# Copying the far maxima directly behind the pairing, with the mark passes and a dense piece moved ahead of the scores

## The chip, the cores and the metric

The kernel runs on one core of a Trainium2 chip. A core has five engines that run side by side, each through its own list of instructions in order: TensorE (PE, matrix products; PEld is its loading of weights), VectorE (DVE), ScalarE (ACT), GpSimd (POOL) and SyncE (SP, which issues transfers here). The metric is the time of one execution in microseconds of device time; lower is better.

## The reference

An attention with a top-32 mask per row, and behind it a feed-forward layer with squared ReLU:

```python
# q, k, v: (8 batches, 8 heads, 576 rows, 64)
scores = q @ k.T / 8
kth = 32nd largest of each row of scores
scores = where(scores >= kth, scores, -1e9)
attn = softmax(scores)
x = (attn @ v) as (4608 tokens, 512)
h = maximum(x @ w_in, 0)         # 512 -> 2048
out = (h * h) @ w_out            # 2048 -> 512
```

## The kernel before

The rows of scores are worked on in 144 steps of two tiles of 128 rows each (`steps`; most steps hold the same chunk of rows of two heads, 16 of them the last 64 rows of four heads). A tile has 576 columns. For each step, in the kernel's names:

- `scores(u)`: TensorE computes the scores into two PSUM tiles, `sc_b` (columns 288 to 575 of the scores) first and then `sc_a` (columns 0 to 287). Each of these tiles has two banks of 512 numbers, one for each of the two tiles of rows, and uses the first 288 of them. ACT copies both to `s` in SBUF (line 202).
- `far` is the place of columns 288 to 431 in the two banks of `sc_b`, behind the scores. It holds the upper half of the pairwise maxima.
- `split(u)`: DVE pairs the two halves of a row: `tops` is the maximum of each pair (line 227). In a step that is *lent* the minima are left to POOL (`small_mins`), and the upper half of the maxima is copied to `far` by ACT (line 209). In a step that isn't lent, DVE writes `far` itself (line 229) and computes half of the minima too. A planner's debts of POOL and ACT decide which steps are lent.
- `join(u)`: DVE pairs `far` with the lower half of `tops` (line 242); in some steps the minima of that are left to POOL (`joint_mins`).
- `topk(u, rounds)`: DVE takes the largest eight of a window and strikes them out, four times (lines 274 and 278). The eighth of the fourth round is the threshold.
- `below(u, x)`: ACT's mark pass, one for each tile of rows (line 320): what lies below the threshold gets a positive mark.
- `exps(u)`: ACT's exponentials (line 328); `mask(u)`: POOL adds the marks to them as integers (line 324); `turn(u)`: a transposing transfer.
- `products(u)`, `invert` and `place(u)`: weighted sums of `v` on TensorE (line 389), reciprocals on DVE (lines 394 and 400), and the scaled copy to `x_tok` on ACT (line 417).
- `dense(u, x)`: one piece of the feed-forward layer on TensorE (lines 494 and 517), or a piece without use where none is ready (line 539); what ACT and POOL do with a piece is issued later, between the exponentials (`flush`).

Every instruction is pinned, so each engine's order is the order in which the code issues it. The steps overlap: in a step u from 12 on (`lead` is 2), the code finishes the top-32 search of step u, pairs the rows of step u + 2, scores those of step u + 3, and works on the marks and exponentials of step u − 1. Where a tile is used by two engines, the framework adds semaphores from the tile's accesses. Steps 9 to 11 (`DEEP` is 9) change over from a lead of 1, in an order of their own. From step 125 on (`Z`) another loop, at line 741, runs the last steps; it has `split` before `topk`, and `ahead`, which issues the scores, behind `mask` and `turn`.

The main loop's order in a step, before the change, cut to the calls that matter:

```python
below(u - 1, 0)
split(u + 2)
ahead(u + 3)            # scores(u + 3), with the copies
topk(u, (0,))
place(f - 1)            # f = u - 4
joint_mins(u + 1)
small_mins(u + 2)
dense(u, 0)
below(u - 1, 1)
topk(u, (1,)); topk(u, (2,)); topk(u, (3,))
join(u + 2)
exps(u - 1); mask(u - 1); turn(u - 1)
dense(u, 1); products(u - 3); prepare(u)
```

Of the kernel before, what the change touches and what calls it, by code (L numbers as in the profile page):

```python
# [17 lines left out]
AF = mybir.ActivationFunctionType  # L18
# [4 lines left out]
def kernel(  # L23
# [9 lines left out]
    nc = tc.nc  # L33
# [10 lines left out]
    HALF, QUAR = S // 2, S // 4  # L44

    def pin(ins):
        tc.keep_in_program_order(ins)
        return ins
# [3 lines left out]
    def owe(**more):  # L52
        for e, t in more.items():
            debt[e] += t

    def pass_step():
        for e in debt:
            debt[e] = max(0.0, debt[e] - {"G": 5.9, "A": 6.1}[e])
# [38 lines left out]
    far = sc[1][:, :, HALF:HALF + QUAR]  # L97
# [82 lines left out]
    Z, DEEP = U - 19, 9  # L180
# [6 lines left out]
    st = {}  # L187


    def scores(u):  # L190
        for j in (1, 0):
            rest = steps[u][0][1] == 4
            for x, g in ((0, 0), (1, 1), (0, 1), (1, 0)) if rest else ((0, steps[u][0][2]), (1, steps[u][1][2])):
                i, c, _ = steps[u][x]
                qkT = prep[i][0]
                r = slice(64 * g, 64 * g + 64)
                pin(nc.tensor.matmul(out=sc[j][r if rest else slice(0, 128), x, 0:HALF], lhsT=qkT[r, 0, c * 128:min(S, (c + 1) * 128)],  # L197
                                     rhs=qkT[r, 1, j * HALF:(j + 1) * HALF], start=True, stop=True))
        s = scp.tile([128, 2, S], f32, name="s", bufs=5)

        def copy(j):
            pin(nc.scalar.activation(s[:, :, j * HALF:(j + 1) * HALF], sc[j][:, :, 0:HALF], AF.Copy))  # L202
        st[u] = {"s": s}
        copy(1)
        if u < 2:
            st[u]["rest"] = lambda: copy(0)
        else:
            if "lent" in st[u - 1]:
                pin(nc.scalar.activation(far, st[u - 1]["tops"][:, :, QUAR:HALF], AF.Copy))  # L209
            copy(0)  # L210
        for i, c, a in steps[u]:
            qk_left[i] -= 1
# [4 lines left out]
    def split(u):  # L217
        d = st[u]
        lend = (2 < u < U - 20 and debt["G"] < 4.9 and debt["A"] < 5.4) or Z < u < U - 5
        cat = d["cat"] = scp.tile([128, 2, S], f32, name="cat", bufs=3)  # L220
        tops = d["tops"] = scp.tile([128, 2, HALF], f32, name="tops", bufs=2)
        one, two = sc[0][:, :, 0:HALF], d["s"][:, :, HALF:S]
        tt = nc.vector.tensor_tensor
        if lend:
            owe(G=1.22, A=0.4)
            d["lent"] = True
            pin(tt(tops[:, :, :], one, two, op=ALU.max))  # L227
        else:
            pin(tt(far, one[:, :, QUAR:HALF], two[:, :, QUAR:HALF], op=ALU.max))
            pin(tt(tops[:, :, 0:QUAR], one[:, :, 0:QUAR], two[:, :, 0:QUAR], op=ALU.max))  # L230
        if not lend:
            pin(tt(cat[:, :, HALF + QUAR:S], one[:, :, QUAR:HALF], two[:, :, QUAR:HALF], op=ALU.min))
        if "rest" in d:
            d.pop("rest")()

    def join(u):
        d = st[u]
        d["joint"] = "lent" in d and DEEP + 4 <= u < Z + 2 and debt["G"] < 4.5
        if d["joint"]:
            owe(G=1.6)  # L240
        for lo, op in ((0, ALU.max), (QUAR, ALU.min))[0:1 if d["joint"] else 2]:
            pin(nc.vector.tensor_tensor(d["cat"][:, :, lo:lo + QUAR], far, d["tops"][:, :, 0:QUAR], op=op))  # L242

    def joint_mins(u):
        d = st[u]
        if d["joint"]:
            at, tops = d["cat"][:, :, QUAR:HALF].bitcast(i32), d["tops"][:, :, :].bitcast(i32)
            pin(nc.gpsimd.tensor_tensor(at, tops[:, :, 0:QUAR], tops[:, :, QUAR:HALF], op=ALU.add))  # L248
            pin(nc.gpsimd.tensor_tensor(at, at, d["cat"][:, :, 0:QUAR].bitcast(i32), op=ALU.subtract))

    def small_mins(u):
        d = st[u]
        n = HALF if "lent" in d else QUAR
        s, at = d["s"], d["cat"][:, :, HALF:HALF + n].bitcast(i32)
        pin(nc.gpsimd.tensor_tensor(at, s[:, :, 0:n].bitcast(i32), s[:, :, HALF:HALF + n].bitcast(i32), op=ALU.add))  # L255
        pin(nc.gpsimd.tensor_tensor(at, at, d["tops"][:, :, 0:n].bitcast(i32), op=ALU.subtract))  # L256
# [61 lines left out]
    def below(u, x):  # L318
        d = st[u]
        pin(nc.scalar.activation(marks[u % 2][:, x, :], d["s"][:, x, :], AF.Relu, bias=d["m"][3][:, x, 7:8], scale=-1.0))  # L320
# [21 lines left out]
    def flush():  # L342
        while late:
            late.pop(0)()
# [191 lines left out]
    def idle_piece(n=KH, name="dn_ps", bufs=1):  # L536
        hp = ps_one.tile([128, 512], f32, name=name, bufs=bufs)
        for kh in range(n):
            pin(nc.tensor.matmul(out=hp[:, :], lhsT=id_h[:, :], rhs=fill[:, :], start=(kh == 0), stop=(kh == n - 1)))
# [3 lines left out]
    def piece():  # L543
        flush()
        turn_of[0] ^= 1
        for q_ in ((ups, downs), (downs, ups))[turn_of[0]]:
            if q_:
                q_.pop(0)()
                return True
        return False  # L550

    def dense(u, x):
        for go in ripe.pop(u, ()):
            go()
        if moves and x == 1:
            flush()
            moves.pop(0)(u)
        if x == 1 and not ups and 0 < len(downs) <= 6 and u < 100:
            flush()
            idle_piece(2, "gen", 2)  # L560
            return
        for n in range(2 if len(ups) + len(downs) > 24 or (x == 1 and u >= 100 and u % 3 == 0 and len(ups) + len(downs) > 4) else 1):
            if not piece() and n == 0 and u < U:
                idle_piece()
# [66 lines left out]
    join(0)  # L631
    small_mins(0)
    scores(1)


    def ok(w):
        return 0 <= w < U
# [11 lines left out]
    def ahead(w):  # L649
        if w < U:  # L650
            for i, c, a in steps[w]:
                while coming <= i or (coming == i + 1 and soon):
                    prepare(u)
            scores(w)

    for u in range(Z):
        f = u - 4
        lead = 2 if u > DEEP + 2 else 1
        pass_step()
        owe(A=4.5, G=3.0)  # L660
        if u > 0:
            below(u - 1, 0)
        if u == 0:
            topk(0, (0, 1))
            split(1)
            join(1)
            topk(0, (2, 3))
        elif not DEEP < u < DEEP + 3:
            split(u + lead)
        if not DEEP < u < DEEP + 3:  # L670
            ahead(u + 1 + lead)
        if u > 0:
            topk(u, (0,))
        if u == DEEP + 2:
            join(u + 1)
            split(u + 2)
            ahead(u + 3)
        if ok(f) and f % 2:
            invert_two(f)
        if ok(f - 1):  # L680
            place(f - 1)
        if checks:
            note()
        if lead > 1:
            joint_mins(u + 1)
        if u == DEEP + 2:
            small_mins(u + 2)
        elif u != DEEP + 1:
            small_mins(u + lead)
        dense(u, 0)  # L690
        if u > 0:
            below(u - 1, 1)
            topk(u, (1,))
            if u == DEEP + 1:
                join(u + 1)
            topk(u, (2,))
            if u == DEEP + 1:
                split(u + 2)
                small_mins(u + 2)
                ahead(u + 3)  # L700
            topk(u, (3,))
            if u == DEEP:
                join(u + 1)
                split(u + 2)
            elif u != DEEP + 1:
                join(u + 2 if u > DEEP else u + 1)
            exps(u - 1)
            mask(u - 1)
            turn(u - 1)
        flush()  # L710
        if u == Z - 1:
            assert u % 2 == 0
            products(u - 3)
            expo(u, 0)
            expo(u, 1)
        else:
            dense(u, 1)
            flush()
            products(u - 3)
        if u == DEEP:  # L720
            small_mins(u + 2)
            ahead(u + 3)
        for _ in range(2 if u < 8 or u in (U - 22, U - 19) else 1):
            prepare(u)
        if 1 < u < 24 and not ups and not downs:
            idle_piece(2)
        turn_x(u)
        if w_casts and u >= 3:
            w_casts.pop(0)()
        if w_loads and u >= 1:  # L730
            w_loads.pop(0)()
# [57 lines left out]
    u = U - 2  # L789
# [67 lines left out]
    u = U - 1  # L857
# [187 lines left out]
```

## Time and profile before

| what | us |
|---|---|
| median of three runs | 907.39 (905.39 to 907.63) |
| the profiled execution | 905.09 |
| its span, from the first to the last instruction | 903.2 |
| VectorE busy | 865.9 |
| ScalarE busy | 827.1 |
| GpSimd busy | 809.7 |
| TensorE busy | 738.5 |

The profile is of one execution. Busy times count the engine's own instructions, without waits. In rows of a timeline the first two numbers are the start and the length in us; a bracket gives idle time before the instruction and what ended it. In rows of waits stand the total of the waits, how many there were and the longest.

### The profile page before, as it was taken

The numbers are of one execution on the slowest core, as the hardware profiler recorded it, in microseconds if no ns is written. First come the engines' busy times: TensorE is split into PE (matmuls) and PEld (weight loads), VectorE is DVE, ScalarE is ACT, GpSimd is POOL, SyncE is SP. The second block draws the span as 40 slices with busy tenths as digits, with TensorE's granted clock in tenths as the row PEclk, the third lists the DMA queues.
The fourth block names the chain that finished last, engine by engine and source line by source line (L and its number), as shares of the span: only waits on it lengthen the run. The fifth ranks groups of instructions, "written<-read, shape, count | busy, mean of one in ns | idle before, by whom it ended". The sixth has DMA issues, their size and how long they took to land.

```text
span 903.2 us, 19114 instructions
## 1 busy us (share of the span) xinstructions
PE 738.5 (82%) x5474; PEld 435.8 (48%) x5474; DVE 865.9 (96%) x3503; ACT 827.1 (92%) x1691; POOL 809.7 (90%) x756
## 2 busy tenths in 40 slices
PE   7888777887778878787888878787888877978986
PEld 3444335455445444454544444455555544545644
DVE  5999889999999999999999999999999999999994
ACT  3988889999999999999999999899999999999973
POOL 4789879999999999999999999999999998899851
PEclk8989889999999898999999999999999998999989
DMA  5597674454566565445554455554546555334431
GB/s 118 136 205 155 167 170 90 99 96 104 100 122 119 96 110 117 88 99 113 108 113 95 101 108 109 109 113 94 112 97 123 114 111 114 68 71 63 89 82 42
DMA packets 326880, 98.00 MB, mean 109 GB/s; under 512 B 318960, under 2 KB 319216, under 8 KB 326768
## 3 DMA queue, kind: packets, MB, share of 16 engines
q1 hardware_dynamic: 325424, 96.28, 52.1%
q8 instruction: 45, 0.74, 0.4%
q10 hardware_dynamic: 1344, 0.43, 0.2%
q14 instruction: 67, 0.55, 0.2%
HBM read 36.70 MB, written 9.44 MB: 51 GB/s over the span
## 4 chain that ended last, share of the span: by engine, by line
DVE 46%; PE 15%; ACT 15%; POOL 9%; issue 8%; DMA 4%; SPq 2%; DVEq 0%; ACTq 0%; POOLq 0%
DVE m L274 18%; DVE cat L278 13%; DVE cat L242 6%; DVE tops L227 6%; ACT s L202 5%; PE sc_b L197 3%; PE av_ps L389 3%; PE dn_ps L517 3%; POOL cat L255 2%; POOL h L503 2%; PE sc_a L197 2%; ACT marks_a L320 2%; POOL cat L256 2%; ACT marks_b L320 1%; ACT x_tok L417 1%
## 5 line engine op out<-in xcount | busy, mean ns | idle before, releaser
L274 DVE MAX8 m<-cat 128x8 f32<-128x104 f32 (+3 forms) x1152 | 437.1, 420 | 0.0
L278 DVE MATCH_REPLACE8 cat<-m,cat 128x104 f32<-128x104 f32 (+2 forms) x864 | 261.2, 309 | 0.0
L256 POOL TENSOR_TENSOR cat<-cat,tops 128x576 int32<-128x576 int32 (+1 forms) x144 | 191.7, 1331 | 13.2 <-DVE tops L230 2.1
L255 POOL TENSOR_TENSOR cat<-s 128x576 int32<-128x576 int32 (+1 forms) x144 | 191.6, 1330 | 7.0 <-ACT s L202 6.6
L389 PEld LDWEIGHTS <-wT 128*128 128x128 bf16 (+3 forms) x1600 | 98.2, 100 | 143.0 <-issue 76.9
L517 PE MATMUL dn_ps<-w_out,h 128*128 128x512 bf16 x560 | 160.0, 417 | 5.2 <-ACT wide L527 5.2
L197 PE MATMUL sc_b<-qkT 64*128 64x288 f32 (+1 forms) x640 | 129.2, 487 | 40.5 <-DVE cat L242 30.5
L503 POOL TENSOR_TENSOR h<-rl 128x512 bf16<-128x512 f32 x140 | 145.0, 1040 | 7.8 <-ACT rl L500 5.4
L494 PEld LDWEIGHTS <-w_in 128*128 128x128 bf16 x1344 | 114.5, 101 | 50.7 <-issue 23.9
L494 PE MATMUL gen<-xT,w_in 128*128 128x256 bf16 (+1 forms) x1088 | 133.0, 271 | 2.6 <-ACT rl L500 1.6
L197 PE MATMUL sc_a<-qkT 64*128 64x288 f32 (+1 forms) x640 | 123.2, 471 | 1.3 <-DVE tops L227 1.3
L242 DVE TENSOR_TENSOR cat<-sc_b,tops 128x288 f32<-128x288 f32 x256 | 104.1, 443 | 10.5 <-ACT sc_b L209 8.5
L320 ACT ACTIVATE marks_a<-s,m 128x576 bf16<-128x576 f32 x144 | 112.0, 786 | 0.4
L202 ACT ACTIVATE s<-sc_b 128x576 f32<-128x576 f32 x144 | 94.1, 654 | 19.5 <-PE sc_b L197 15.0
L320 ACT ACTIVATE marks_b<-s,m 128x576 bf16<-128x576 f32 x142 | 109.2, 776 | 0.1
L202 ACT ACTIVATE s<-sc_a 128x576 f32<-128x576 f32 x144 | 91.7, 637 | 7.9 <-PE sc_a L197 5.3
L227 DVE TENSOR_TENSOR tops<-sc_a,s 128x576 f32<-128x576 f32 x126 | 94.0, 746 | 1.3 <-POOL cat L248 1.0
L517 PEld LDWEIGHTS <-h 128*128 128x128 bf16 x560 | 51.3, 104 | 83.3 <-issue 43.5
L197 PEld LDWEIGHTS sc_b<-qkT 64*128 64x128 f32 (+1 forms) x640 | 50.6, 186 | 71.8 <-DVE cat L242 40.0
L500 ACT ACTIVATE rl<-gen 128x512 f32<-128x512 f32 x140 | 83.3, 595 | 1.7 <-PE gen L494 1.2
L197 PEld LDWEIGHTS sc_a<-qkT 64*128 64x128 f32 (+1 forms) x640 | 61.5, 196 | 40.2 <-DVE tops L227 21.1
L328 ACT ACTIVATE w_two_a<-s,low 128x576 bf16<-128x576 f32 x96 | 71.5, 774 | 0.8
(136 smaller groups left out, 1170.5 us busy)
## 6 DMA issues: line engine op xcount, KB each, us to landing
q_raw<-in_q_dram SPq DMA_DIRECT2D x64, 128.0 KB, 3.0
v_raw<-in_v_dram SPq DMA_DIRECT2D x64, 128.0 KB, 3.1
k_raw<-in_k_dram SPq DMA_DIRECT2D x62, 128.0 KB, 3.0
out_dram<-wide SPq DMA_DIRECT2D x31, 256.0 KB, 2.7
h<-in_moe_w_in_dram SPq DMA_DIRECT2D x8, 512.0 KB, 5.2
h<-in_moe_w_out_dram SPq DMA_DIRECT2D x8, 512.0 KB, 4.3
out_dram<-wide SPq DMA_DIRECT2D x9, 128.0 KB, 2.4
q_raw<-in_q_dram SPq DMA_DIRECT2D x32, 32.0 KB, 2.8
```

The lines of the kernel that those rows point to most:

```text
L197: pin(nc.tensor.matmul(out=sc[j][r if rest else slice(0, 128), x, 0:HALF], lhsT=qkT[r, 0, c * 128:min(S, (c + 1) * 128)], rhs=qkT[r, 1, j ...
L202: pin(nc.scalar.activation(s[:, :, j * HALF:(j + 1) * HALF], sc[j][:, :, 0:HALF], AF.Copy))
L227: pin(tt(tops[:, :, :], one, two, op=ALU.max))
L242: pin(nc.vector.tensor_tensor(d["cat"][:, :, lo:lo + QUAR], far, d["tops"][:, :, 0:QUAR], op=op))
L255: pin(nc.gpsimd.tensor_tensor(at, s[:, :, 0:n].bitcast(i32), s[:, :, HALF:HALF + n].bitcast(i32), op=ALU.add))
L256: pin(nc.gpsimd.tensor_tensor(at, at, d["tops"][:, :, 0:n].bitcast(i32), op=ALU.subtract))
L274: pin(nc.vector.max(out=m[r][:, x, :], in_=cat[:, x, at]))
L278: pin(nc.vector.match_replace(out=cat[:, x, at], in_to_replace=m[r][:, x, :], in_values=cat[:, x, at], imm_value=NEG))
L320: pin(nc.scalar.activation(marks[u % 2][:, x, :], d["s"][:, x, :], AF.Relu, bias=d["m"][3][:, x, 7:8], scale=-1.0))
L494: pin(nc.tensor.matmul(out=hp[:, n * n_rows:(n + 1) * n_rows], lhsT=w_in[:, kh, (f0 + n) * 128:(f0 + n + 1) * 128], rhs=xt(kh), start=(kh ...
L503: squares.append(lambda by: pin(by.tensor_mul(h2, flat, flat)))
L517: pin(nc.tensor.matmul(out=op[:, :], lhsT=held["h2"][:, f, c * 128:(c + 1) * 128], rhs=w_out[:, f, :], start=(f == 0), stop=(f == NF - 1)))
```

## The change

Three things move; no instruction is added or taken out.

- The copy of the upper maxima to `far` is issued in `split`, directly behind the pairing, for all lent steps from 11 on. It stood in `scores` of the next step, between the copies of `sc_b` and `sc_a`.
- From step 12 on both mark passes stand at the head of the step.
- From step 12 on `joint_mins`, `small_mins` and the first dense piece stand directly behind `split`, ahead of the scores.

```diff
         if u < 2:
             st[u]["rest"] = lambda: copy(0)
         else:
-            if "lent" in st[u - 1]:
+            if "lent" in st[u - 1] and u - 1 < DEEP + 2:
                 pin(nc.scalar.activation(far, st[u - 1]["tops"][:, :, QUAR:HALF], AF.Copy))
             copy(0)
...
             pin(tt(tops[:, :, :], one, two, op=ALU.max))
+            if u >= DEEP + 2:
+                pin(nc.scalar.activation(far, tops[:, :, QUAR:HALF], AF.Copy))
...
         if u > 0:
             below(u - 1, 0)
+        if lead > 1:
+            below(u - 1, 1)
...
         elif not DEEP < u < DEEP + 3:
             split(u + lead)
+        if lead > 1:
+            joint_mins(u + 1)
+            small_mins(u + 2)
+            dense(u, 0)
         if not DEEP < u < DEEP + 3:
             ahead(u + 1 + lead)
...
-        if lead > 1:
-            joint_mins(u + 1)
         if u == DEEP + 2:
             small_mins(u + 2)
-        elif u != DEEP + 1:
+        elif lead == 1 and u != DEEP + 1:
             small_mins(u + lead)
-        dense(u, 0)
+        if lead == 1:
+            dense(u, 0)
         if u > 0:
-            below(u - 1, 1)
+            if lead == 1:
+                below(u - 1, 1)
             topk(u, (1,))
```

## The prediction

> **What bounds the kernel now.** I read the page first, then the busy times of stretches of the span.
>
> ```profile
> span 903.2 us, 19114 instructions
> ## 1 busy us (share of the span) xinstructions
> PE 738.5 (82%) x5474; PEld 435.8 (48%) x5474; DVE 865.9 (96%) x3503; ACT 827.1 (92%) x1691; POOL 809.7 (90%) x756
> ```
>
> VectorE (DVE) has the most work, but ScalarE (ACT) and GpSimd (POOL) are close. The shares are diluted by the start and the end, so I asked for the stretch from 75 to 850 us, which holds nearly everything that the change touches (columns: stretch, length, busy PE, PEld, DVE, ACT, POOL with counts, granted clock, DMA share, GB/s).
>
> ```profile
> 75.00:850.00 775.00, 633.99 (x4715) 376.95 (x4713) 761.62 (x3097) 741.61 (x1523) 736.74 (x666) 0.93 0.53 106
> ```
>
> There DVE is idle for 775.00 − 761.62 = 13.4 us and ACT for 775.00 − 741.61 = 33.4 us. So DVE sets the pace and ACT follows closely: whatever lengthens ACT's in-order list by more than 33.4 us in all makes ACT the bound. How much could the change win? The far copy is L209, and DVE's only large wait in this stretch is for it, in the join of L242:
>
> ```profile
> DVE cat L242 <- ACT sc_b L209: 8.5, 10, 2.3
> ```
>
> Ten waits, 8.5 us. That is the most that an earlier far copy can give.
>
> Next, one step on ACT, in order of time (start, length).
>
> ```profile
> 401.62 0.77 ACT L320 ACTIVATE marks_b<-s,m 128x576 bf16<-128x576 f32 x1
> 402.29 0.64 ACT L202 ACTIVATE s<-sc_b 128x576 f32<-128x576 f32 x1
> 402.96 0.41 ACT L209 ACTIVATE sc_b<-tops 128x288 f32<-128x288 f32 x1
> 403.31 0.63 ACT L202 ACTIVATE s<-sc_a 128x576 f32<-128x576 f32 x1
> 403.84 0.51 ACT L417 ACTIVATE x_tok<-av_ps,shares 128x64 bf16<-128x64 f32 x2
> 404.23 0.78 ACT L320 ACTIVATE marks_b<-s,m 128x576 bf16<-128x576 f32 x1
> ```
>
> Nothing here waits: each starts before the last has quite ended. The same step on DVE (the join, then the pairing of the next rows) and on TensorE (scores, then a dense piece):
>
> ```profile
> 399.66 0.43 DVE L242 TENSOR_TENSOR cat<-sc_b,tops 128x288 f32<-128x288 f32 x1
> 400.01 0.74 DVE L227 TENSOR_TENSOR tops<-sc_a,s 128x576 f32<-128x576 f32 x1
> ...
> 405.14 0.80 DVE L242 TENSOR_TENSOR cat<-sc_b,tops 128x288 f32<-128x288 f32 x2
> ...
> 405.86 0.74 DVE L227 TENSOR_TENSOR tops<-sc_a,s 128x576 f32<-128x576 f32 x1
> ```
>
> ```profile
> 400.14 0.76 PE L197 MATMUL sc_b<-qkT 64*128 64x288 f32 x4 [0.28 <-DVE cat L242]
> 400.81 0.76 PE L197 MATMUL sc_a<-qkT 64*128 64x288 f32 x4
> 401.50 1.04 PE L517 MATMUL dn_ps<-w_out,h 128*128 128x512 bf16 x4
> ```
>
> Pairing starts at 400.01 and again at 405.86: a step of 5.85 us. Its tops are ready at 400.75, ACT's first mark pass starts only at 401.62: ACT runs behind DVE and finds its inputs ready.
>
> Now the point that decides. The scores of sc_b go to columns 0 to 287 of a bank; "far" is columns 288 to 431 of the same bank. Still TensorE starts those scores 0.05 us after the join, which only reads far, has ended (399.66 + 0.43 = 400.09). That is the rule over the whole kernel (idle time before line 197, times):
>
> ```profile
>   DVE cat L242: 70.5, 90
> ```
>
> And where DVE writes far itself, in a step that isn't lent, the scores come 0.05 us behind the end of that write (376.22 + 0.47 = 376.69), before the next two DVE operations:
>
> ```profile
> 376.22 0.47 DVE L229 TENSOR_TENSOR sc_b<-sc_a,s 128x288 f32<-128x288 f32 x1
> ...
> 376.74 0.76 PE L197 MATMUL sc_b<-qkT 64*128 64x288 f32 x4
> ```
>
> So in this program whoever touches far holds back the scores of sc_b, and the scores hold back whoever comes next, although no byte is shared. The Trainium skill, "PSUM — Partial Sum Buffer", section "PSUM bank collisions raise a hardware error", goes further than these two rows: any two engines on one bank must be ordered by semaphores, writes and reads alike, even for different columns. No row here shows scores behind an ACT write to far; by that rule they wait for it too and the time would be the forecast's 1021, and if only shared bytes counted, the 897 of the first rival.
>
> **The change, part by part.** No instruction is added or removed; the order on ACT, PE and POOL changes.
>
> *The far copy.* Before, ACT ran: sc_b copy of the next scores, far copy, sc_a copy. The scores had been computed long before, under the mark pass. Now the far copy stands before the scores in program order, so I expect the chain: far copy, then scores of sc_b, then the sc_b copy, and ACT has nothing between the first and the last. The list on ACT becomes mark, mark, far copy, (wait), sc_b copy, sc_a copy, x_tok. From the start of the far copy to the start of the sc_a copy: 0.41 for the copy, 0.05 to release TensorE, 0.76 for the scores of sc_b, 0.05 back to ACT, and 0.67 until the sc_a copy can start, since sc_a's scores end 401.57 − 400.90 = 0.67 us behind sc_b's. Sum 1.94 us. Before, sc_b copy, far copy and sc_a copy took 403.31 − 402.29 = 1.02 us to the same point. The step's ACT list grows by 0.92 us. From below: if the sc_a copy could follow after 0.53 us (403.31 to 403.84), it is 0.78.
>
> How often:
>
> ```profile
> 75.00:850.00 775.00, 48.92 (x118) 0.93 0.53 106
> ```
>
> This row is line 209's alone: 118 far copies in the stretch. Three of them belong to steps 9 to 11, whose order is another one; I count 115: 115 × 0.92 = 105.8 us (from below 115 × 0.78 = 89.7).
>
> *Steps of remainders.* By the list of steps, 16 of the 144 score the last 64 rows of four heads with twice the matmuls; two lie before step 9 and two follow a step that isn't lent, which leaves 12. One of them:
>
> ```profile
> 476.97 2.19 PE L197 MATMUL sc_b<-qkT 64*64 64x288 f32 x8 [1.97 <-DVE cat L242]
> 478.94 1.72 PE L197 MATMUL sc_a<-qkT 64*64 64x288 f32 x8
> ```
>
> The scores of sc_b take 2.19 instead of 0.76, and sc_a's end 480.66 − 479.16 = 1.50 behind them instead of 0.67: 1.43 + 0.83 = 2.26 us more on ACT. This row is a long one; I take 2.0: 12 × 2.0 = 24 us. From below 0.
>
> *Scores at a lower clock.* The row of the stretch grants 0.93, and such a group looks like this:
>
> ```profile
> 413.10 1.33 PE L197 MATMUL sc_b<-qkT 64*128 64x288 f32 x4
> 414.22 1.17 PE L197 MATMUL sc_a<-qkT 64*128 64x288 f32 x4
> ```
>
> If a stretch at half clock makes 0.93 out of 1, its share is 14%, and each such step costs 0.57 for sc_b and 0.49 for sc_a's later end (1.16 instead of 0.67): at most 115 × 0.14 × 1.06 = 17 us. These groups are hidden today and the rows at 400.14 and 376.74 have 0.76, so I take half, 8 us; the ends are 0 and 17.
>
> *What ACT gets back.* Once ACT is the bound, its waits of today fall into the new one. In the stretch (busy, mean ns | idle before and its releasers, then two waits):
>
> ```profile
> L202 ACT ACTIVATE s<-sc_b 128x576 f32<-128x576 f32 x130 | 85.1, 654 | 11.7 <-PE sc_b L197 7.2 <-ACT marks_a L320 2.0 <-issue 1.5
> L202 ACT ACTIVATE s<-sc_a 128x576 f32<-128x576 f32 x129 | 82.1, 636 | 5.0 <-PE sc_a L197 5.0
> ```
>
> ```profile
> ACT w_out L590 <- DMA h<-in_moe_w_out_dram: 7.0, 2, 3.9
> ...
> ACT qkT L132 <- PE gen L128: 1.4, 4, 0.5
> ```
>
> 11.7 + 5.0 + 1.4, and half of the 7.0, since data that a later ACT asks for has had more time to land: 21.6 us, say 22. The ends are 17 (the copies' waits alone) and 33 (all of ACT's idle time).
>
> *The mark pass moved ahead.* Its maxima are there, as ACT trails DVE, so it waits for nothing. It delays both copies by 0.67 us. The sc_b copy is needed by the pairing at 405.86 and ended at 402.93, 2.9 us early. Behind the second mark (0.67), the far copy (0.41) and the wait (0.86) it ends 1.94 us later, 1.0 us early. That cover shrinks with each step in which ACT falls behind: it costs nothing extra, it is where the 0.92 reaches DVE.
>
> *The dense piece ahead of the scores.* 1.04 us on TensorE. It runs while ACT does its two mark passes and the far copy (0.67 + 0.67 + 0.41 = 1.75 us), so scores don't wait for it: nothing. If that cover is gone, up to 1.04 us a step. Behind the x_tok copies TensorE has the weighted sums and transposes, then this piece; ACT has two exponentials, up to two activations of pieces, two marks and the far copy, which is longer.
>
> *POOL's two passes.* They now stand ahead of the overflow notes, eight small groups; their order against the masks and squares is kept. Nothing. No DMA is issued by anything moved, so SP's queue passes nothing.
>
> *The win.* At most the 8.5 us of the join's waits; it is DVE's idle time, and DVE no longer sets the end. I count nothing.
>
> The profiled execution took 905.1 us, 1.9 more than its span, and 2.3 less than the median of the runs. Sum: 905.1 + 105.8 + 24 + 8 − 22 = 1020.9, **1021 us**. Check against ACT alone: (741.6 + 33.4 − 22 + 137.8) = 891 us for the stretch, against DVE's 762: ACT is the bound by far. From below: 905.1 + 89.7 − 33 = 962. From above: 905.1 + 105.8 + 12 × 2.26 + 17 − 17 = 1038.
>
> **The rivals.** *The scores don't wait for the far copy.* If the program orders ACT's write and the matmul by columns, the far copy comes earlier or as early as now, ACT gains no wait, and the join's 8.5 us go: 905.1 − 8.5 = 896.6. For it: the join reads far in steps where scores are still to come. Against it: the 90 waits for the join and the row at 376.74, both without a shared byte. It decides if a matmul on sc_b starts while line 209 still runs. Chance 5%.
>
> *ACT's slack takes the wait.* ACT idles 33.4 us over some 130 steps, 0.26 us a step; a wait of up to that would be free and the time would stay 905. It takes a wait of 0.92 to shrink below 0.3, which the 0.76 of the scores alone excludes unless TensorE starts early. Chance 3%.
>
> *The clock falls.* If TensorE's new gaps make half clock more frequent, say in 40% of the time instead of 14%, the scores cost 115 × 0.26 × 1.06 = 32 us more: 1053, and more with a larger share. For it: the granted clock isn't 1 today. Against it: the gaps per step are under 1 us, and today's waits of TensorE at x_tok are as long or longer. The Trainium skill, "TensorE: Matmul & The Clock Gate", section "A second HAM failure mode: psum-queue depth-cycling", has frequent short idle times between groups of matmuls as a cause of an oscillating clock; by that this rival would hold, with its 1053, and today's 0.93 neither shows nor excludes it. Chance 8%.
>
> **How the numbers follow.** The forecast, 1021, has 84%. Its own ends are 962 and 1038; the clock rival adds up to 1053. The range is 960 to 1055. A measurement here tells about 0.3% from no change, 2.7 us: faster 0.05 (the first rival), same 0.03 (the second), slower 0.92 (the forecast and the clock).
>
> **What would show it.** In the profile of the changed kernel: the scores of sc_b wait for ACT at line 209's copy, about a hundred times; the sc_b copy of ACT idles some 100 us for TensorE's scores, against 11.7; DVE has a new idle time of 80 to 130 us in the join or the pairing, released by ACT's sc_b copy or the scores, and its share falls to about 85%; the step grows from 5.9 to about 6.8 us; the granted clock stays at 0.9 or above. I am wrong if line 209's copy and the scores overlap, if ACT's idle time stays at some 33 us in this stretch, or if the far copy's wait is for the pairing instead.

## The result: 13% slower, and the profile after

The changed kernel takes 1028.74 us (median of four, 1024.22 to 1033.26) against 907.51 us for the kernel before in the same comparison: a ratio of 1.134 (95% interval 1.127 to 1.141), 121 us more. The profiled execution took 1024.2 us. In line numbers after, the far copy is L229, the join L244; the pairing is still L227 and the copies of the scores L202.

The page of the changed kernel, its first lines:

```profile
span 1022.2 us, 18810 instructions
## 1 busy us (share of the span) xinstructions
PE 753.5 (74%) x5397; PEld 450.2 (44%) x5474; DVE 880.0 (86%) x3503; ACT 826.0 (81%) x1691; POOL 811.9 (79%) x756
```

ACT has the work that it had (826.0 after 827.1 us), and DVE nearly (880.0 after 865.9). So the loss is nearly all idle time: over the span ACT's went from 76.1 to 196.2 us and DVE's from 37.3 to 142.2 us, in a span that is 119.0 us longer. The question is who waits first. One step on ACT, which answers to the six rows shown of before:

```profile
462.56 1.43 ACT L322 ACTIVATE marks_b<-s,m 128x576 bf16<-128x576 f32 x2
463.89 0.40 ACT L229 ACTIVATE sc_b<-tops 128x288 f32<-128x288 f32 x1
465.21 0.65 ACT L202 ACTIVATE s<-sc_b 128x576 f32<-128x576 f32 x1 [0.92 <-PE sc_b L197]
465.75 0.65 ACT L202 ACTIVATE s<-sc_a 128x576 f32<-128x576 f32 x1
466.29 0.52 ACT L419 ACTIVATE x_tok<-av_ps,shares 128x64 bf16<-128x64 f32 x2
```

and on TensorE, with a dense piece that ended before the wait:

```profile
461.87 1.03 PE L519 MATMUL dn_ps<-w_out,h 128*128 128x512 bf16 x4
464.35 0.76 PE L197 MATMUL sc_b<-qkT 64*128 64x288 f32 x4 [1.45 <-ACT sc_b L229]
464.94 0.65 PE L197 MATMUL sc_a<-qkT 64*128 64x288 f32 x4
```

and on DVE:

```profile
465.89 0.82 DVE L244 TENSOR_TENSOR cat<-sc_b,tops 128x288 f32<-128x288 f32 x2 [1.05 <-ACT s L202]
466.63 0.75 DVE L227 TENSOR_TENSOR tops<-sc_a,s 128x576 f32<-128x576 f32 x1
```

ACT's far copy ends at 464.29, the scores start 0.06 us later, and the sc_b copy starts 0.92 us after the far copy's end. ACT does nothing in between. TensorE has nothing to do either: its dense piece is long done. The chain of before (the scores early, under a mark pass) has turned into far copy, scores, copy, one behind the other.

The four longest waits of the kernel (engine, line and what released it: us in total, times, longest):

```profile
PEld sc_b L197 <- ACT sc_b L229: 227.8, 118, 3.6
PE sc_b L197 <- ACT sc_b L229: 178.1, 112, 3.1
ACT s L202 <- PE sc_b L197: 135.0, 123, 2.4
DVE cat L244 <- ACT s L202: 99.5, 97, 2.9
```

They are the chain in its order: scores behind the far copy, 118 times; ACT behind the scores, 135.0 us; DVE's join behind ACT, 99.5 us. The wait of 8.5 us that the join had for the far copy is gone, and 99.5 us have come in its place.

The last link is easy to overlook. The join reads `far` and `tops`; it needs nothing of the sc_b copy. Yet it starts at 465.89, 0.03 us after that copy's end (465.21 + 0.65), and all 94 joins of the kernel that had idled for over 0.3 us start as close behind an sc_b copy. So the place of `far` ties two engines to the scores of sc_b: TensorE doesn't write them before the far copy, and DVE doesn't read `far` before ACT has read them.

The stretch of the moved copies now goes from 75 to 960 us:

```profile
75.00:960.00 885.00, 644.10 (x4559) 385.60 (x4622) 764.55 (x3047) 729.90 (x1501) 729.45 (x656) 0.90 0.46 93
```

ACT is idle for 885.00 − 729.90 = 155.1 us there, against 33.4 us in the stretch of before: 121.7 us more, the size of the loss. DVE's idle time went from 13.4 to 120.5 us. By the groups of ACT in this stretch, the two copies of the scores now hold 143.3 us of it, after 16.7:

```profile
L202 ACT ACTIVATE s<-sc_b 128x576 f32<-128x576 f32 x128 | 83.2, 650 | 130.8 <-PE sc_b L197 130.1 <-ACT marks_a L322 0.3
L202 ACT ACTIVATE s<-sc_a 128x576 f32<-128x576 f32 x128 | 83.0, 648 | 12.5 <-PE sc_a L197 12.4
```

### The profile page after: what moved, and what is told of

Read it like the earlier page. It is cut to its first block, busy times and chain, and to the rows that moved or that the text cites. A ratio compares the mean times of both kernels' runs of the same rounds, so it can differ in the third digit from the quotient of the medians.

```text
span 1022.2 us, 18810 instructions
## 1 busy us (share of the span) xinstructions
PE 753.5 (74%) x5397; PEld 450.2 (44%) x5474; DVE 880.0 (86%) x3503; ACT 826.0 (81%) x1691; POOL 811.9 (79%) x756
## 4 chain that ended last, share of the span: by engine, by line
ACT 37%; PE 22%; DVE 19%; POOL 12%; issue 8%; DMA 1%; SPq 1%; ACTq 0%; POOLq 0%; DVEq 0%
PE sc_b L197 9%; ACT s L202 7%; DVE m L276 6%; ACT marks_a L322 6%; ACT marks_b L322 6%; DVE cat L280 4%; DVE tops L227 4%; PE sc_a L197 4%; ACT rl L502 4%; POOL cat L257 3%; PE av_ps L391 3%; ACT sc_b L229 3%; DVE cat L244 3%; POOL cat L258 2%; ACT w_two_b L330 2%
## 5 line engine op out<-in xcount | busy, mean ns | idle before, releaser
L197 PE MATMUL sc_b<-qkT 64*128 64x288 f32 (+1 forms) x640 | 134.8, 509 | 187.0 <-ACT sc_b L229 178.1
L202 ACT ACTIVATE s<-sc_b 128x576 f32<-128x576 f32 x144 | 93.6, 650 | 137.0 <-PE sc_b L197 135.0
L244 DVE TENSOR_TENSOR cat<-sc_b,tops 128x288 f32<-128x288 f32 x256 | 106.1, 451 | 100.1 <-ACT s L202 99.5
L519 PE MATMUL dn_ps<-w_out,h 128*128 128x512 bf16 x496 | 142.0, 405 | 14.2 <-issue 6.3
L496 PE MATMUL gen<-xT,w_in 128*128 128x256 bf16 (+1 forms) x1088 | 144.6, 284 | 8.5 <-ACT rl L502 7.0
L391 PEld LDWEIGHTS <-wT 128*128 128x128 bf16 (+3 forms) x1600 | 102.5, 103 | 99.7 <-issue 59.9
L496 PEld LDWEIGHTS <-w_in 128*128 128x128 bf16 x1344 | 117.1, 104 | 61.1 <-issue 41.1
L197 PE MATMUL sc_a<-qkT 64*128 64x288 f32 (+1 forms) x640 | 119.9, 463 | 0.0
L202 ACT ACTIVATE s<-sc_a 128x576 f32<-128x576 f32 x144 | 93.3, 648 | 15.8 <-PE sc_a L197 12.7
L322 ACT ACTIVATE marks_a<-s,m 128x576 bf16<-128x576 f32 x144 | 105.7, 794 | 0.0
L227 DVE TENSOR_TENSOR tops<-sc_a,s 128x576 f32<-128x576 f32 x126 | 94.5, 750 | 12.3 <-ACT s L202 8.9
L322 ACT ACTIVATE marks_b<-s,m 128x576 bf16<-128x576 f32 x142 | 102.4, 769 | 0.1
L197 PEld LDWEIGHTS sc_a<-qkT 64*128 64x128 f32 (+1 forms) x640 | 68.3, 205 | 26.2 <-issue 3.4
```

Of the source, the lines that this page charges most:

```text
L496: pin(nc.tensor.matmul(out=hp[:, n * n_rows:(n + 1) * n_rows], lhsT=w_in[:, kh, (f0 + n) * 128:(f0 + n + 1) * 128], rhs=xt(kh), start=(kh ...
L519: pin(nc.tensor.matmul(out=op[:, :], lhsT=held["h2"][:, f, c * 128:(c + 1) * 128], rhs=w_out[:, f, :], start=(f == 0), stop=(f == NF - 1)))
```

## The experiments

The theory: the far copy shares banks with the scores of sc_b, so these wait for it; ACT, which waits for the scores, has nothing to do in between, and as it has no slack for 0.9 us a step, it becomes the bound. The rivals: the moved order costs by itself; an early far copy costs by itself; or TensorE's clock and time do.

### Half of the change: the far copy alone

```diff
-            if "lent" in st[u - 1]:
+            if "lent" in st[u - 1] and u - 1 < DEEP + 2:
                 pin(nc.scalar.activation(far, st[u - 1]["tops"][:, :, QUAR:HALF], AF.Copy))
...
             pin(tt(tops[:, :, :], one, two, op=ALU.max))
+            if u >= DEEP + 2:
+                pin(nc.scalar.activation(far, tops[:, :, QUAR:HALF], AF.Copy))
```

> Only the far copy is moved into the pairing; mark passes, small minima and dense piece stay where they were. Theory (scores of sc_b wait for the far copy's bank, and ACT waits for them with nothing in between): ACT again runs far copy, wait of about 0.9 us, sc_b copy, so most of the 121 us stays: 1000 to 1035 us, with the sc_b copies of ACT idle for 100 to 140 us until the scores. Rival (the moved mark pass and dense piece are what costs, since they delay the scores and both copies): 895 to 910 us.

1059.7 us, ratio 1.167 (1.163 to 1.172). The far copy alone makes the whole loss and 31 us more than the change, above the range that I had given. ACT's waits:

```profile
ACT s L202 <- PE sc_b L197: 142.7, 125, 2.4
ACT qkT L132 <- PE gen L128: 30.6, 28, 3.0
```

The first is the chain. The second, 30.6 us after 9.0 in the changed kernel, is new: the transposes that prepare the next heads come late. That is taken up below.

### The other half: the order alone

The change without the two hunks above: marks, POOL minima and the dense piece moved, the far copy in its old place.

> Only the order is changed (both mark passes, the POOL minima and the first dense piece ahead of the scores); the far copy stays between the two copies of the scores. Theory: the scores wait for nothing new, and the copies have cover: 900 to 920 us, the sc_b copies idle for under 30 us. Rival (the order is the cost): 1000 us or more.

918.6 us, ratio 1.014 (1.010 to 1.018): 12 us slower, not 121. The scores wait for nothing new, as expected. What the order costs stands in DVE's waits, 8.5 us before:

```profile
DVE cat L242 <- ACT sc_b L209: 20.3, 20, 3.4
```

The second mark pass now stands ahead of the copies, so the far copy behind them comes later for the join: 11.8 us more, the size of the loss. (DVE's idle time over the span grows by as much, from 37.3 to 49.0 us.)

### Far in SBUF: the bank taken away, and another wait in its place

```diff
-                pin(nc.scalar.activation(far, tops[:, :, QUAR:HALF], AF.Copy))
+                d["far"] = cat[:, :, QUAR:HALF]
+                pin(nc.scalar.activation(d["far"], tops[:, :, QUAR:HALF], AF.Copy))
...
-            pin(nc.vector.tensor_tensor(d["cat"][:, :, lo:lo + QUAR], far, d["tops"][:, :, 0:QUAR], op=op))
+            pin(nc.vector.tensor_tensor(d["cat"][:, :, lo:lo + QUAR], d.get("far", far), d["tops"][:, :, 0:QUAR], op=op))
```

> The whole change, order and all, but in the lent steps the far copy goes to a part of cat in SBUF that is free until the join, and the join reads it there: the number of instructions is the same and only the bank is not shared. Theory (the shared bank is the whole cost): the wait of the scores for the copy is gone, 895 to 920 us, if the join from SBUF takes its 0.44 us; each 0.1 us more of a join adds 20 to 25 us. Rival (the early copy or the order costs by itself, in ACT's time or TensorE's clock): 990 us or more.

1027.2 us, ratio 1.134 (1.130 to 1.138), the number of the rival, and within 2 us that of the change. But the rows are not the rival's. ACT's wait for the scores of sc_b, and the page's busy times:

```profile
ACT s L202 <- PE sc_b L197: 12.9, 15, 1.5
```

```profile
PE 781.3 (76%) x5474; PEld 439.9 (43%) x5474; DVE 995.5 (97%) x3503; ACT 828.7 (81%) x1691; POOL 849.0 (83%) x756
```

The chain is gone, 12.9 us after 135.0, and DVE is the bound with 995.5 us of work. Its join is what grew (duration min/median/max in ns, from SBUF and, in the steps that aren't lent, from PSUM):

```profile
L245 DVE TENSOR_TENSOR cat<-cat,tops x204: 429/1177/1697, 75.4 to 958.9; 128x288 f32<-128x288 f32 x102
L245 DVE TENSOR_TENSOR cat<-sc_b,tops x52: 432/447/466, 10.5 to 992.2; 128x288 f32<-128x288 f32 x52
```

1177 ns with both inputs in SBUF against 447, and 429 at best: the operation isn't slower in itself. The Trainium skill, "SBUF — State Buffer", section "Who interferes with whom", says that a DVE instruction with two SBUF inputs contends with a GpSimd instruction that reads SBUF; GpSimd is busy for 83% of this span, so the rows agree. Two joins and the GpSimd instruction beside the second:

```profile
466.37 1.92 DVE L245 TENSOR_TENSOR cat<-cat,tops 128x288 f32<-128x288 f32 x2
466.71 1.26 POOL L506 TENSOR_TENSOR h<-rl 128x512 bf16<-128x512 f32 x1
```

The second join ends at 468.29, 0.32 us after the GpSimd instruction's end at 467.97. All 162 joins of this group that took over 0.6 us end 0.31 to 0.32 us after the end of a GpSimd instruction, and the 12 with under 0.1 us of GpSimd beside them took 431 to 459 ns. So the join is held until GpSimd is done.

As a test of the shared bank this run settles half: without it the scores don't wait. It doesn't show what the time would be, since the cure costs as much. The next but one does.

### The wait covered: far copy first, then both mark passes

```diff
-            below(u - 1, 0)
-            below(u - 1, 1)
             split(u + 2)
+            below(u - 1, 0)
+            below(u - 1, 1)
             joint_mins(u + 1)
             small_mins(u + 2)
             dense(u, 0)
             ahead(u + 3)
```

(cut to the calls that matter; in the main loop from step 12 on, and likewise in the loop of the last steps).

> The change, but with the pairing and its far copy at the head of the step and both mark passes behind them, so that ACT has 1.34 us of marks to do while TensorE waits for the copy and computes the scores. Theory (the cost is that ACT has nothing to do in the 0.9 us between far copy and sc_b copy): the wait is covered, 895 to 912 us, the sc_b copies idle for under 30 us, the join's wait for the far copy gone. Rival (TensorE's later scores or a lower clock cost by themselves): 950 us or more, with the scores still waiting for the far copy.

914.2 us, ratio 1.0076 (1.0054 to 1.0098), 2 us over the expected range. One step of ACT:

```profile
503.65 0.46 ACT L229 ACTIVATE sc_b<-tops 128x288 f32<-128x288 f32 x1
503.98 1.48 ACT L322 ACTIVATE marks_a<-s,m 128x576 bf16<-128x576 f32 x2
505.31 0.69 ACT L202 ACTIVATE s<-sc_b 128x576 f32<-128x576 f32 x1
505.84 0.70 ACT L202 ACTIVATE s<-sc_a 128x576 f32<-128x576 f32 x1
```

The scores still start behind the far copy (59.8 us of TensorE's waits are for it), but ACT spends that time on marks, and its waits for them are 16.7 us instead of 135.0. The order of three ACT instructions decides about 114 of the 121 us. It still doesn't beat the kernel before. The sc_b copy comes late for the join, which waits 13.9 us for it; but the profiled execution took 907.8 us, the shortest of the five, so these rows don't show where the 7 us of the median go.

### Far behind the scores of sc_a

```diff
-    far = sc[1][:, :, HALF:HALF + QUAR]
+    far = sc[0][:, :, HALF:HALF + QUAR]
```

> The whole change, but far lies behind the scores of sc_a, in the banks that the pairing has just read, instead of behind those of sc_b. Every instruction and its place in the order is that of the change. Theory (whose bank is shared decides): the scores of sc_b no longer wait for the far copy and the sc_b copy follows it at once; the scores of sc_a now wait for it, but the sc_b copy of 0.65 us covers most of those 0.92 us: the wait is 0.2 to 0.3 us a step, more in the steps of remainders: 908 to 945 us. Rival (an early far copy or the moved order costs by itself): 990 us or more.

938.3 us, ratio 1.035 (1.032 to 1.038), within the theory's range. One name is changed, no instruction and no place in the order, and 90 of the 121 us are gone:

```profile
505.46 0.40 ACT L229 ACTIVATE sc_a<-tops 128x288 f32<-128x288 f32 x1
505.79 0.64 ACT L202 ACTIVATE s<-sc_b 128x576 f32<-128x576 f32 x1
506.77 0.65 ACT L202 ACTIVATE s<-sc_a 128x576 f32<-128x576 f32 x1 [0.34 <-PE sc_a L197]
```

Now the sc_b copy follows the far copy at once, and the wait sits before the sc_a copy, 0.34 us long, as the sc_b copy covers the rest. Which bank is shared decides, not that the copy is early. The remaining loss is the same chain in small: ACT waits 43.3 us for the scores of sc_a, and the join, which now reads `far` out of sc_a, waits 42.9 us. Of its waits of over 0.3 us, 37 end right behind the sc_a copy, none behind the sc_b copy: the join's wait has moved with `far`, too.

A tile of scores is two banks here, and the semaphores come from the accesses to tiles. No run separates "the same tile" from "the same bank"; the runs show that the place of `far` decides, and "bank" in this text stands for both.

### The scores of sc_b twice over, after and before

```diff
+                for again in range(2 if j and u > DEEP + 4 and not rest else 1):
                     pin(nc.tensor.matmul(out=sc[j][r if rest else slice(0, 128), x, 0:HALF], ...
```

In the changed kernel:

> The change, with the scores of sc_b computed twice over in each step of four matmuls from step 15 on, to the same place. Theory (they lie on ACT's path between far copy and sc_b copy): the wait grows by their own length, 0.6 to 0.76 us in some 110 steps, so 1028 + 66 to 84, 1090 to 1115 us. Rival (they are covered by other work and the time comes from elsewhere): under 1045 us.

1079.1 us, ratio 1.189 (1.185 to 1.193): 50 us more than the change, less than the 66 to 84 that I had expected. In the kernel before:

> The same doubling in the kernel before. Theory (there the scores are ready long before ACT comes to copy them): little of it shows, 905 to 935 us. Rival (TensorE's time counts in full in both kernels): 970 us or more.

914.5 us, ratio 1.008 (1.005 to 1.011): 7 us. So the same matmuls cost seven times as much after the change, which is what being on the path means. The size was off because I took the length of the group (0.76 us) for the cost of the second; the wait of a usual step shows it:

```profile
509.56 0.44 ACT L230 ACTIVATE sc_b<-tops 128x288 f32<-128x288 f32 x1
511.42 0.65 ACT L203 ACTIVATE s<-sc_b 128x576 f32<-128x576 f32 x1 [1.42 <-PE sc_b L198]
```

1.42 us instead of 0.92: a second group adds 0.50 us. In the list of waits ACT's total for these scores rises from 135.0 to 188.1 us, 53 us and so about the loss.

### One mark pass and the x_tok copies under the wait

```diff
             split(u + 2)
             below(u - 1, 0)
-            below(u - 1, 1)
             joint_mins(u + 1)
             small_mins(u + 2)
             dense(u, 0)
-            ahead(u + 3)
             topk(u, (0,))
...
             place(f - 1)
+            ahead(u + 3)
+            below(u - 1, 1)
```

> Pairing and far copy at the head of the step, then one mark pass and the two x_tok copies of ACT, then the two copies of the scores, then the other mark pass: between far copy and sc_b copy ACT has about 1.06 us to do, more than the 0.92 us of the wait and less than the 1.34 us of the version with both marks, so that the sc_b copy comes earlier for the join. Theory: the wait stays covered and the join waits less than 13.9 us in all: 895 to 910 us. Rival (the x_tok copies wait for DVE's reciprocals and hold ACT up): 912 us or more.

914.3 us, ratio 1.0078 (1.0059 to 1.0098): as long as the version with both marks, and outside what the theory gave. The wait stays covered (ACT's waits for the scores of sc_b are 20.7 us) and the join's wait fell, but to 11.7 us only. It is a miss as a better version; ACT's waits for the reciprocals are 3.0 us, after 3.6 in the changed kernel, so the rival isn't shown either. Why these two stay 7 us above the kernel before is open: the join's waits, 11.7 and 13.9 us against 8.5, would be 3 to 5 us of it.

### Why the far copy alone is slower than the whole change

Two versions of the change, each with one move taken back. First the dense piece behind the scores again:

```diff
             small_mins(u + 2)
-            dense(u, 0)
             ahead(u + 3)
...
+            dense(u, 0)
```

> The change, but with the first dense piece back behind the scores (marks, far copy and POOL minima as in the change). It asks why the far copy alone took 32 us more than the whole change. If the dense piece is what gave that back (it fills TensorE's wait for the far copy; behind the scores it comes late for the sums and transposes that ACT then waits for): 1050 to 1070 us, ACT's waits for the transposes 15 to 30 us, clock under 0.88. If the mark pass gave it back: 1025 to 1035 us.

1108.4 us, ratio 1.224 (1.219 to 1.228), slower than both cases. Then the second mark pass back behind the x_tok copies:

> The change, but with the second mark pass back behind the x_tok copies (dense piece, far copy and POOL minima as in the change). If the dense piece gave the 32 us back: 1020 to 1035 us. If the mark pass did: 1050 to 1070 us. ACT's list has the same content in both cases, and the wait between far copy and sc_b copy stays near 0.92 us.

1029.0 us, ratio 1.136 (1.132 to 1.140): the time of the change. So, with the far copy moved, it is the dense piece that matters: with the new place of the mark pass, having it ahead of the scores saves 1108.4 − 1028.7 = 80 us. With the old place of the mark pass the difference is 1059.7 − 1029.0 = 31 us; but the far copy alone has POOL's minima in their old place, too, so that these 31 us are not the dense piece's for certain. The mark pass's place is worth nothing when the dense piece stands ahead (1029.0 against 1028.7); when it doesn't, the new place comes with 49 us more, again with the minima moved as well. TensorE in the version at 1108 us:

```profile
499.37 0.66 PE L128 MATMUL gen<-id_f,k_raw 128*128 128x128 f32 x4
502.34 0.76 PE L197 MATMUL sc_b<-qkT 64*128 64x288 f32 x4 [2.31 <-ACT sc_b L229]
502.93 0.65 PE L197 MATMUL sc_a<-qkT 64*128 64x288 f32 x4
503.52 1.86 PE L519 MATMUL dn_ps<-w_out,h 128*128 128x512 bf16 x4
505.17 1.92 PE L496 MATMUL gen<-xT,w_in 128*128 128x256 bf16 x8
```

It stands still for 2.31 us, and then both dense pieces come at once, ahead of the sums and transposes. ACT, which has waited for the scores of sc_b (147.9 us in all), waits again: for the transposes, for the scores of sc_a and for a dense piece:

```profile
ACT qkT L132 <- PE gen L128: 37.1, 38, 2.8
ACT s L202 <- PE sc_a L197: 22.0, 67, 1.2
ACT rl L502 <- PE gen L496: 21.0, 27, 1.8
```

37.1, 22.0 and 21.0 us, after 9.0, 12.7 and 2.4 us in the changed kernel. The granted clock is 0.848 here, 0.860 with the far copy alone, 0.893 with the dense piece ahead and 0.908 in the changed kernel, so part of this is slower matmuls: the dense pieces above take 1.86 and 1.92 us instead of 1.03 and 1.05, with a granted clock of 0.52 and 0.50 in these two stretches. How much is clock and how much is order isn't separated by these runs.

## Why the prediction was right, step by step

- **The bank as the deciding point** was right. I had read it from waits for the join and from one DVE write (the 90 waits are 52 of weight loads and 38 of matmuls, so they stand for fewer than 90 steps); the scores wait for ACT's write in the same way, 118 times. The section of the Trainium skill cited there asks for such an order between any two engines on the same partitions of one bank; the trace agrees, as no group of scores overlaps a far copy. The run with far in sc_a's banks shows that the place of `far` decides, and the run with far in SBUF that without a shared bank the scores don't wait.
- **0.92 us a step** was nearly right. From far copy to sc_a copy it is 465.75 − 463.89 = 1.86 us in the step above, against 1.94 forecast and 1.02 before: 0.84 more. The wait before the sc_b copy is 0.92 us, which is also its median in the stretch, where I had 0.86; that this wait and the forecast growth both read 0.92 is chance. The sc_a copy follows after 0.54 us, not 0.67: the scores of sc_a start 0.59 us after those of sc_b.
- **The remainders and the lower clock**: I gave 24 and 8 us, 32 together. Counted in ACT's idle time beyond 0.92 us a step, before both copies, the 12 steps of remainders cost 15 us and the usual steps whose scores ran at a lower clock 19. The sum is right, but by luck: the one was 9 us too high and the other 11 too low. The remainder that I had taken for all, 2.19 us at 476.97, ran at a granted clock of 0.50. Another in the kernel before, at a clock of 1.00, takes 1.19 us:

```profile
689.55 1.19 PE L197 MATMUL sc_b<-qkT 64*64 64x288 f32 x8 [0.49 <-DVE cat L242]
```

In the changed kernel 8 of the 12 wait only 1.35 us before the sc_b copy, 0.44 more than a usual step. In the clock's own term I had also misread a row: sc_a's scores end 415.39 − 414.43 = 0.96 us behind sc_b's there, not 1.16, which makes the forecast of that term, and of the clock rival, still lower.
- **What ACT gets back** I put at 22 us. The copies' old waits, 16.7 us, did go over into the new ones: 143.3 − 16.7 = 126.6 us more before the copies, 121.7 us more in all, so that the other waits gave back 4.9 us, where I had 22 − 16.7 = 5.3.
- **The sum**, 1021 us, is 8 us under the median and 3 us under the profiled execution. In idle time of ACT it was 105.8 + 24 + 8 − 22 = 115.8 us; the trace has 118 steps × 0.92 = 108.6 us, 15 for the remainders, 19 for the lower clock and 21.6 given back, together 121 of the 121.7 us. So the main term and the give-back were right by their reasons, and the two in between were right only together.
- **The mark pass and the dense piece "for nothing"** was right for the change as a whole, but not for the reason given alone. By itself the order costs 12 us, through the join's wait for the far copy, which the whole change doesn't have. And the dense piece isn't neutral: with it behind the scores the change would be 80 us slower still, 0.7 us a step. I had priced only what it could cost ahead of the scores, and not that behind them it comes late for the sums and transposes.
- **The bound changes**: DVE falls to 86% (85 forecast), waits 99.5 us for ACT in the join and 120.5 in all (80 to 130). I had the sc_b copy as needed by the pairing, 1.0 us early; it is the join before the pairing that it holds, 97 times, and the pairing 24 times (8.9 us). The pairings of two steps in a row start at 459.62, 466.63 and 472.62, 7.0 and 6.0 us apart (6.8 forecast).
- **The rivals.** That the scores don't wait for the far copy is excluded by the 118 waits. That ACT's slack would take the wait would have needed a far shorter one; the version with the marks under it shows how: not slack but other work covers it. The clock fell a little, from 0.92 to 0.91 over the profiled span. It didn't decide: the usual step has its wait of 0.92 us with scores that take 0.76 us, as before.

## What to carry to other kernels

Before moving a producer earlier, ask who is held back by it: here the copy's own consumer could gain 8.5 us at most, and a matmul that merely shares its bank lost its head start. A chain that goes from an in-order engine to another and back (copy, matmul, copy) costs the first engine the whole round trip, 0.92 us here, unless independent work stands between the two ends in its list; put that work there, or put the two on different banks. And compare an engine's idle time a step (0.26 us) with the wait that you add to it before you count on slack. And before you take a row for the size of an operation, read the granted clock of its stretch.

## What the runs showed that I had not expected

A join with both inputs in SBUF took 1177 ns in the median against 447 with one input in PSUM, held until a GpSimd instruction beside it ended. That by itself made DVE the bound, at the very time of the change: a run that matches a rival's number need not match its cause.

The granted clock, 0.923 before and 0.908 after the change, was lowest, 0.860 and 0.848, in the two versions with the dense piece behind the scores. There TensorE's waits for the far copy average 2.0 and 2.2 us, against 1.6 us or less in the other profiles. Below that the clock doesn't follow these waits: at 1.6 us it is 0.908 in the changed kernel and 0.925 with the doubled scores, at 1.4 us 0.893 with the mark pass in its old place, and in the kernel before, without such waits, 0.923. I had put the clock's fall down as a rival that adds to the change; it came clearly only where the dense piece was behind the scores, and why is not shown.
